# Another written order for the first 48 steps of attention → rational FFN → relu² FFN, with dummy matmuls in front of 16 groups on TensorE

## The chip, the cores and the metric

One core of one Trainium2 chip. Its engines are named as the profile names them: PE (TensorE matmul) with its weight loads PEld, DVE (VectorE), ACT (ScalarE), POOL (GpSimd) and SP (SyncE, which here only issues DMAs). The metric is the device time of one launch in microseconds; lower is better. Before the change it is 1639.45 us, the median of three runs (1637.97 to 1639.97).

## The reference

Three stages, all in float32 accuracy (the FFN weights arrive as float64):

```python
# attention in chunks of 64 tokens; 8 batches x 8 heads, 576 tokens, head dim 64
scores = (q_c @ k_c.T) / sqrt(64);  scores -= max(scores)
attn = exp(scores) / (sum(exp(scores)) + 1e-9);  x = attn @ v_c      # -> 4608 x 512
# FFN 1, rational; w_in 512 x 2048, w_out 2048 x 512
h = x @ w_in
g = (a0 + a1*h + a2*h**2 + a3*h**3) / (1 + |b0|*|h| + |b1|*h**2 + 1e-6)
x = g @ w_out
# FFN 2, relu squared
x = (s * relu(x @ w_in2)**2 + b) @ w_out2
```

## The kernel before, in words

Attention is done in *units* of 128 tokens. A unit n goes through these steps, each one letter of an order list: `P`/`L` load q, k and v; `T` transposes q and k on PE; `q`, `k` copy them out of PSUM on ACT; `S` makes the scores on PE; `sa`, `sb` (row maxima) and `sc`, `sd` (subtract) on DVE; `e` the exponential on ACT; `ma` to `mc` the sum and its reciprocal on DVE; `n` the normalisation, on POOL, or on DVE where it is written `nD`; `A` a transpose on PE and `a` its copy on ACT; `V` the product with v on PE; `v` the high part of the result on ACT (line 416) and `u` the low part on DVE (line 424). From unit 8 on, `X` transposes q and k on DVE (line 327) in place of `T`. Four units make a block of 512 tokens.

A number is kept as a high part and a low part, so a product is three PE passes. The weights of FFN 1 are prepared tile by tile (16 tiles of each matrix): `w` loads a float64 tile, `f` takes its words apart on ACT (lines 445 and 449), `ga` to `gd` join two tiles' bits on DVE (456, 460, 463), `c` adds on POOL (466), `d` makes the high part on ACT, and the low part (477) is made on DVE (`D`) or POOL (`G`).

A *step* i of FFN 1 is one token block with one 128-column tile of the hidden layer: `M` (lines 530 to 532, twelve 128x512 matmuls), then on three engines `B`, `t`, `l`, `E`, `H` (ACT), `ba`, `bb`, `Na`, `Nb`, `Nc` (DVE: 657, 659, 679, 681, 683), the denominator `r` (634 and 637 on POOL; `p` puts its first half on ACT), the low part `y` of the result (697, on POOL, or on DVE as `yD`), and `R` (line 548, twelve matmuls with w_out). Three PSUM banks hold the hidden values, so `M` of step i waits for `Nc` of step i-3. Steps 0 to 7 use token block 0, 8 to 15 block 1, and step 16 is the first of block 2, which needs units 8 to 11.

Nothing schedules at run time: each engine works through its instructions in program order, and that order is written out by hand-made lists. `START` covers steps 0 to 47 and units 0 to 16; after it `LOOP` covers steps 48 to 127, and `TURN` and a planner cover the change to FFN 2. `play(START)` walks the list and calls the function of each letter; each engine's instruction order is the order in which its letters stand. A letter may end in a mark that names an engine or, for PE groups, the PSUM banks.

Of the kernel before, what the change touches and what calls it, by code (L numbers as in the profile page):

```python
# [33 lines left out]
    "w0 w1A f0 P4 w2 f1 P1 g1Pa g1Pb g1Pc c0 d0 T4a L1A T1x q1 k1 g1Pd D0 f2 S1y s1b c1 d1 w3 q4 s1d s1a k4 w4 w5 "  # L34
    "f3 P3 S4b s1c e1 s4b g3Pa g3Pb s4d T3d G1 g3Pc g3Pd m1a c2 m1b m1c P2 f4 c3 n1D f5 w6A d2 g5Pa P5 q3 s4a g5Pb "
    "P0 d3 s4c w7 g5Pc x0 e4 m4a g5Pd A1a k3 T2b c4 c5 a1 V1a S3x q2 s3b k2 d5 s3a d4 G3 s3c S2b s3d e3 w8 v1 D4 "
    "s2b L4 u1 T5d s2a G2 k5 G5 q5 L3A T0x q0 w9 s2c k0 S5a m4b S0x m4c s2d s5a n4 s5b f6 m3a P6 m3b A4d a4 s5c w10 "
    "s0a m3c s0b s5d f7 V4d s0d L0 g7Pa n3 f8 g7Pb g7Pd s0c e2 e5 A3b m5a P7A e0 f9 a3 g7Pc v4 T6b m0a q6 m5b g9Pa "
    "m5c V3c k6 c6 g9Pb n5D m2a w11 g9Pc m0b u4 m0c w12 n0D w13 Q8 c8 A5b S6a s6b L5 L2A c7 L6 T7b w14 d6 a5 w15 "
    "m2b d7 v3 m2c k7 q7 g9Pd s6a c9 s6d s6c e6 D7 m6a A0d u3 a0 d8 w16 Q9 d9 n2 S7b m6b G6 A2a a2 V2a s7a m6c f10 "  # L40
    "v2 u2 V0c v0 L7 G8 f11 u0 M0 w17 f12 g11Pa o8 M1 o9 g11Pb w18 f13 g11Pc G9 g11Pd t0 n6 c11 w19 g13Pa B0 c10 p0 "
    "r0h Q10 A6c d11 M2 s7b w20 b0a g13Pb t1 B1 p1 W0 b0b X8 b1a l0 V5a r1h E0 g13Pc s7c c12 s7d b1b e7 t2 S8b M3 "
    "N0a d10 l1 d12 s8a G11 a6 G12 m7a v5 B2 N0b f14 m7b E1 D10 N0c m7c b2a u5 n7 A7x b2b g13Pd r2 H0 s8b V6a M4 "
    "N1a s8d y0 f15 N1b v6 s8c l2 N1c t3 u6 H1 c13 g15Pa E2 b3a Q11 R0 B3 d13 N2a e8 a7 y1 g15Pb N2b D13 M5 N2c r3 "
    "B4 X9 p4 r4h t4 b3b R1 l3 M6 g15Pc g15Pd c14 H2 l4 y2 E3 f16 b4a N3a f17 b4b E4 N3b V7y c15 B5 p5 r5h m8a d14 "
    "G14 N3c g17Pa H3 t5 d15 B6 l5 y3 v7 R2 N4a N4b m8b t6 N4c g17Pb o10 b5a m8c b5b E5 n8 u7 g17Pd A8c c17 p6 r6h "
    "N5a a8 H4 N5b w21A M7 f18 l6 Q12 B7 f19 d17 S9y o11 D15 N5c g17Pc y4D c16 H5 s9a b6a s9c g19Pa b6b G17 s9b E6 "
    "R3 d16 p7 r7h g19Pb t7 y5D M8 g19Pc R4 t8 N6a b7a N6b s9d B8 X10 G16 l7 b8a N6c f20 f21 r8 o12 R5 g19Pd M9 c19 "
    "e9 b7b H6 E7 b8b g21Pa N7a t9 y6 B9 c18 m9a l8 N7b p9 r9h E8 N7c w22A H7 d19 g21Pb R6 m9b g21Pc M10 b9a d18 "
    "N8a l9 b9b c20 N8b m9c B10 y7D g21Pd E9 t10 N8c p10 N9a R7 M11 b10a c21 j7 i7 H8 N9b B11 b10b S10b N9c V8a n9 "  # L50
    "O7 r10h y8 w23A d21 s10a s10b X11 l10 s10c A9y v8 M12 s10d a9 e10 u8 V9b G18 S11a E10 t11 m10a N10a H9 G19 r11 "
    "w24 m10b v9 w25 w26 m10c B12 N10b n10 N10c s11a o13 l11 s11b s11d s11c Q13 u9 b11a f22 e11 d20 m11a f23 t12 "
    "m11b b11b E11 A10y H10 g23Pa M13 b12a r12 g23Pb m11c a10 t13 N11a N11b B13 R8 y9 l12 R9 N11c g23Pd V10y y10 "
    "n11 R10 g23Pc v10 M14 H11 A11x c23 b12b b13a p13 r13h E12 u10 b13b l13 N12a M15 E13 N12b t14 N12c y11 B14 D20 "
    "R11 H12 c22 d22 N13a a11 N13b N13c y12 V11y R12 b14a d23 t15 b14b w27A r14 H13 b15a l14 B15 D23 E14 N14a G22 "
    "v11 G21 u11 N14b M16 M17 r15 N14c b15b f24 f25 g25Pa l15 g25Pb y13D E15 g25Pd B16 r16 N15a f26 g25Pc R13 t16 "
    "f27 N15b M18 N15c g27Pa B17 H14 y14 b16a b16b H15 p17 r17h l16 t17 b17a E16 b17b N16a N16b l17 y15D c25 c24 "
# [24 lines left out]
)
# [1530 lines left out]
```

## Time and profile before

| | |
|---|---|
| median of 3 runs | 1639.45 us |
| the profiled execution's own time | 1639.77 us |
| its span | 1638.0 us |
| PE busy | 1586.5 us (97%) |
| DVE, ACT, POOL busy | 82%, 69%, 37% of the span |
| step 0 starts on PE | 60.84 us |
| step 48 starts on PE | 353.0 us |

The span is what the hardware profiler saw of one execution, from the first instruction to the last; the time around it (1.8 us) is launch and end. "Busy" is the union of an engine's instructions. Matmuls are pipelined and their ends modelled, so the distance between two starts says more than a duration: in a dense stretch one 128x512 matmul starts 0.227 us after the other, and a step (`M` and `R`) takes 5.44 us of PE. The column PEclk is the clock granted to TensorE as a share of full speed; its two levels are 1.2 and 2.4 GHz.

### The profile page before, as it was taken

The page shows a single profiled execution, that of the slowest core. Times are in us where ns is not written, and L with a number is a line of the kernel's source. Part 1 is how long each engine was busy: PE and PEld are TensorE (multiplying, and loading weights), DVE is VectorE, ACT ScalarE, POOL GpSimd, SP SyncE. Part 2 cuts the span into 40 slices and gives each one's busy share as a digit, 9 for nine tenths or more (in the row PEclk, how much of TensorE's full clock was granted, in tenths as well). Part 3 has the DMA queues.
Part 4 walks back from the last instruction along what each step waited for, and adds up shares of the span by engine and source line. Part 5 has one row for each costly group of instructions (what it writes and reads, how often), then busy time and mean ns, then how long its engine had stood idle before and what let it go on. Part 6 is the DMA issues. An engine that isn't in the chain of part 4 may idle for free.

```text
span 1638.0 us, 26407 instructions
## 1 busy us (share of the span) xinstructions
PE 1586.5 (97%) x9068; PEld 1293.9 (79%) x9068; DVE 1338.1 (82%) x2165; ACT 1128.0 (69%) x1909; POOL 608.8 (37%) x513
## 2 busy tenths in 40 slices
PE   4699999999999999999999999999999999999998
PEld 3577887777878888888888788888888888888886
DVE  6899988899888988888779987668867886788676
ACT  5788766667677686867678776657665756676554
POOL 3677565347577676757557510000000000000000
PEclk9799999999999999999999999999999999999999
DMA  9655302344263553625034587865589649666853
GB/s 232 158 158 147 93 1 65 84 113 134 66 167 87 154 141 83 196 65 133 3 123 135 206 272 238 324 231 174 164 208 303 233 130 297 213 220 161 279 169 86
DMA packets 365526, 263.93 MB, mean 161 GB/s; under 512 B 276816, under 2 KB 315728, under 8 KB 364880
## 3 DMA queue, kind: packets, MB, share of 16 engines
q1 hardware_dynamic: 352720, 255.55, 53.0%
q10 hardware_dynamic: 12672, 6.69, 1.5%
q8 instruction: 72, 1.18, 0.3%
q14 instruction: 62, 0.51, 0.1%
HBM read 201.33 MB, written 60.82 MB: 160 GB/s over the span
## 4 chain that ended last, share of the span: by engine, by line
PE 79%; DVE 6%; DMA 4%; ACT 4%; issue 3%; POOL 2%; SPq 2%; ACTq 0%; DVEq 0%; POOLq 0%
PE acc L548 20%; PE ae L1107 16%; PE hA L1046 11%; PE h L530 7%; PE h L532 6%; PE h L531 6%; PE hE L1046 5%; PE hc L1046 3%; PE hc L1107 3%; DMA wst<-in_moe_w_in_dram 1%; SPq L269 1%; DMA vs<-in_v_dram 1%; PE pat L383 1%; DVE ah L679 1%; PE pat L408 1%
## 5 line engine op out<-in xcount | busy, mean ns | idle before, releaser
L1107 PE MATMUL ae<-gs,wo 128*128 128x512 f32 x1152 | 294.0, 391 | 1.7 <-DVE acc L1126 0.7
L548 PE MATMUL acc<-gh,w 128*128 128x512 f32 x1152 | 288.0, 392 | 0.0
L530 PE MATMUL h<-xh,w 128*128 128x512 f32 x640 | 256.1, 400 | 8.9 <-DVE t L683 8.0
L1107 PEld LDWEIGHTS ae<-gs,wo 128*128 128x128 f32 x1152 | 215.8, 188 | 49.5 <-DVE acc L1126 1.1
L531 PE MATMUL h<-xl,w 128*128 128x512 f32 x640 | 251.0, 392 | 0.0
L532 PE MATMUL h<-xh,w 128*128 128x512 f32 x640 | 251.0, 392 | 0.0
L548 PEld LDWEIGHTS acc<-gh,w 128*128 128x128 f32 x1152 | 214.1, 188 | 44.4 <-ACT gh L691 0.2
L637 POOL TENSOR_TENSOR r<-r,ah 128x512 f32<-128x512 f32 x130 | 174.3, 1341 | 77.6 <-ACT r L632 65.0
L1046 PE MATMUL hA<-xs,wi 128*128 128x512 f32 x768 | 195.6, 390 | 0.7 <-ACT g L1057 0.7
L697 POOL TENSOR_TENSOR gl<-t,gh 128x512 fp32r<-128x512 f32 x111 | 147.7, 1333 | 100.0 <-ACT gh L691 58.4
L1046 PEld LDWEIGHTS hA<-xs,wi 128*128 128x128 f32 x768 | 144.1, 188 | 31.8 <-ACT g L1057 1.1
L1085 DVE TENSOR_TENSOR gs<-g,gs 128x512 fp32r<-128x512 f32 x224 | 146.4, 684 | 15.1 <-ACT gs L1081 14.5
L548 PE MATMUL acc<-gl,w 128*128 128x512 f32 x576 | 154.8, 390 | 2.0 <-POOL gl L697 1.9
L1081 ACT ACTIVATE gs<-g 128x512 fp32r<-128x512 f32 x224 | 132.7, 624 | 28.2 <-DVE g L1077 27.8
L530 PEld LDWEIGHTS h<-xh,w 128*128 128x128 f32 x640 | 121.2, 189 | 39.1 <-DVE t L683 12.4
L532 PEld LDWEIGHTS h<-xh,w 128*128 128x128 f32 x640 | 121.0, 189 | 26.0
L531 PEld LDWEIGHTS h<-xl,w 128*128 128x128 f32 x640 | 121.2, 189 | 24.2 <-DVE xl L424 0.3
L623 ACT ACTIVATE t<-h,a_sb 128x512 f32<-128x512 f32 x144 | 111.1, 773 | 38.1 <-PE h L532 18.1
L548 PEld LDWEIGHTS acc<-gl,w 128*128 128x128 f32 x576 | 107.6, 188 | 26.5 <-POOL gl L697 4.2
L679 DVE SCALAR_TENSOR_TENSOR ah<-r,h 128x512 f32<-128x512 f32 x144 | 98.1, 681 | 37.1 <-ACT h L668 35.7
L1128 DVE TENSOR_TENSOR acc<-ae,acc 128x512 f32<-128x512 f32 x112 | 77.0, 689 | 61.3 <-PE ae L1107 60.3
L663 ACT ACTIVATE ah<-r,lnb 128x512 f32<-128x512 f32 x144 | 103.6, 719 | 32.8 <-POOL r L637 26.5
(143 smaller groups left out, 2964.9 us busy)
## 6 DMA issues: line engine op xcount, KB each, us to landing
wi<-wq SPq DMA_DIRECT2D x112, 512.0 KB, 4.3
wo<-wq SPq DMA_DIRECT2D x112, 512.0 KB, 4.8
wst<-in_moe_w_in_dram SPq DMA_DIRECT2D x28, 512.0 KB, 5.3
wst<-in_moe_w_out_dram SPq DMA_DIRECT2D x27, 512.0 KB, 4.7
wi<-wp SPq DMA_DIRECT2D x16, 512.0 KB, 4.0
wq<-wc SPq DMA_DIRECT2D x32, 256.0 KB, 2.8
w<-wi SPq DMA_DIRECT2D x16, 512.0 KB, 6.6
raw<-x2d SPq DMA_DIRECT2D x16, 512.0 KB, 7.4
```

Source lines behind the costliest of these rows:

```text
L530: T.matmul(h, wh, xh[:, kk], start=kk == 0, stop=False)
L531: T.matmul(h, wh, xl[:, kk], start=False, stop=False)
L532: T.matmul(h, wl, xh[:, kk], start=False, stop=kk == KD - 1)
L548: T.matmul(o, l, r, start=first and n == 0, stop=last and n == 2)
L623: A.activation(t1, h_t[i], AF.Identity, scale=a_sb[:, 3:4], bias=a_sb[:, 2:3])
L637: eng.tensor_tensor(out=r, in0=r, in1=ah, op=ALU.mult)
L679: V.scalar_tensor_tensor(out=t, in0=r, scalar=ONE, in1=y, op0=ALU.add, op1=ALU.mult)
L697: (eng or (G if i < N1 else V)).tensor_tensor(out=gl, in0=tmp.pop(i)["g"], in1=f(g_t[i][0]), op=ALU.subtract)
L1046: T.matmul(ps[b], w[:, l, z * P:(z + 1) * P], x[:, z], start=n == 0 and p in (1, 2, 5), stop=n == 5, skip_group_check=True)
L1081: A.activation(gx[t, s, k][0][:, 0], gt[t, s, c], AF.Copy)
L1085: V.tensor_tensor(out=g[:, 1], in0=gt[t, s, c], in1=f(g[:, 0]), op=ALU.subtract)
L1107: T.matmul(o, w[:, e, l, dp * P:(dp + 1) * P], gx[t, 2 * u + e, k][0][:, g], start=n == 0 and p in (1, 2, 5), stop=n == 5, skip_group_chec ...
```

## The change

The text of `START` is replaced by another order of nearly the same letters. Some letters change their mark, which moves work between engines. Counted over the whole list: `D` (weight low part on DVE) 13 → 6 and `G` (on POOL) 19 → 26; `nD` 6 → 1 and `n` 11 → 16; `yD` 15 → 10 and `y` 32 → 37; `p` (first half of the denominator on ACT) 19 → 13 and `r` on POOL alone 25 → 31; v loads issued from ACT (`LA`) 3 → 0, of 4 DMAs each; the parameters' load `x` moves from the middle of the first loads to the front of SP's queue. The second of the two ACT operations of `f` (line 449) becomes a letter of its own, `h…b`. New is `+`: so many transposes of the identity by itself into a PSUM bank that nothing reads, 172 in 16 groups (26, 31, 1, 17, 6, 6, 6, 10, 9, 6, 3, 9, 8 and 12 ahead of step 0, 20 ahead of step 3 and 2 in front of the first `R`).

```diff
 START = (
-    "w0 w1A f0 P4 w2 f1 P1 g1Pa g1Pb g1Pc c0 d0 T4a L1A T1x q1 k1 g1Pd D0 f2 S1y s1b c1 d1 w3 q4 s1d s1a k4 w4 w5 "
...
+    "w0A w1A x0 f0 h0b f1 P1 g1Pa h1b g1Pb g1Pd +26c T1b w2 f2 g1Pc w3 k1 c0 f3 c1 P2 w4 q1 g3Pa d1 g3Pb h3b d0 "
+    "+31c T2d h2b S1a k2 q2 w5 D0 g3Pd f4 g3Pc f5 h5b P0 G1 h4b P5 +1h S2b s1a +17c T0d s1b s1c s1d q0 g5Pa P4 w6 "
...
+    def heat(n, x):
+        if x in "ab":
+            to = ps_a.tile([P, 2, TB], F32, tag=f"acc{'ab'.index(x)}", name="heat")[:, 0]
+        elif x == "x":
+            to = ps_a.tile([P, TB], F32, tag="att", name="heat")
+        else:
+            to = h_bank("cdh".index(x))
+        for _ in range(n):
+            T.transpose(to[:, 0:P], ident, ident)
...
-            w_ends(st, w)
+            w_abs(st, w)
+            if phase:
+                w_low(st)
...
-        do["h"] = lambda n, _: w_get(n)
+        do["h"] = lambda n, x: w_low(words[n][3]) if x else w_get(n)
```

The lines of the new kernel stand 7 to 11 lower, so line 477 is 484 there, 316 is 327, and so on.

PE, from the program's start, before (line 316 is `T`, 339 is `S`, 383 is `A`; `h` and `pat` are PSUM banks):

```order
L316 MATMUL pat<-ident,qk 128x128 x12
L316 MATMUL h<-ident,qk 128x128 x4
L339 MATMUL pat<-qk,vq 64x64
L339 MATMUL h<-qk,vq 64x64 x2
L339 MATMUL pat<-qk,vq 64x64 x2
```

PE at the same place, now (line 319 is the new dummy transposes, 327 is `T`, 350 is `S`):

```order
L319 MATMUL h<-ident 128x128 x26
L327 MATMUL pat<-ident,qk 128x128 x8
L319 MATMUL h<-ident 128x128 x31
L327 MATMUL h<-ident,qk 128x128 x8
L350 MATMUL pat<-qk,vq 64x64 x16
L319 MATMUL h<-ident 128x128
L350 MATMUL pat<-qk,vq 64x64 x16
L319 MATMUL h<-ident 128x128 x17
```

The dummies need only `ident`, which is made at the start, and stand in front of groups that wait for a load.

DVE, the end of the first attention units, before (368, 371 and 373 are `ma`, `mb`, `mc`, 377 is `nD`):

```order
L463 SCALAR_TENSOR_TENSOR w<-wst,w 128x512 x2
L368 TENSOR_REDUCE sm<-e 128x8
L371 TENSOR_SCALAR sm<-sm 128x8
L373 RECIPROCAL sm<-sm 128x8
L377 TENSOR_TENSOR e<-e,sm 128x512
```

DVE at the end of the first attention units, now (379, 382 and 384 are `ma`, `mb`, `mc`, 360 and 367 are the maxima and subtractions of other units):

```order
L379 TENSOR_REDUCE sm<-e 128x8
L382 TENSOR_SCALAR sm<-sm 128x8
L367 TENSOR_TENSOR e<-pat,mx 128x4x64 x2
L384 RECIPROCAL sm<-sm 128x8
L379 TENSOR_REDUCE sm<-e 128x8
L360 TENSOR_REDUCE mx<-pat 128x4 x2
```

The normalisation no longer follows the reciprocal on DVE; it stands on POOL.

POOL, around the first results of the steps, before (634 and 637 are `r`, 697 is `y`, 466 is `c`, 377 is `n`, 477 is `G`):

```order
L634 TENSOR_SCALAR r<-ah,ab_sb 128x512
L637 TENSOR_TENSOR r<-r,ah 128x512
L697 TENSOR_TENSOR gl<-t_878,gh 128x512
L466 TENSOR_TENSOR w<-w,wst 128x512
L697 TENSOR_TENSOR gl<-t_934,gh 128x512
L634 TENSOR_SCALAR r<-ah,ab_sb 128x512
L637 TENSOR_TENSOR r<-r,ah 128x512 x2
L466 TENSOR_TENSOR w<-w,wst 128x512
L697 TENSOR_TENSOR gl<-t_974,gh 128x512
```

POOL at the first results of the steps, now (641 and 644 are `r`, 704 is `y`, 473 is `c`, 388 is `n`, 484 is `G`):

```order
L641 TENSOR_SCALAR r<-ah,ab_sb 128x512
L644 TENSOR_TENSOR r<-r,ah 128x512
L484 TENSOR_TENSOR w_7_1271<-w,w_7_1271 128x512
L704 TENSOR_TENSOR gl<-t_1084,gh 128x512
L704 TENSOR_TENSOR gl<-t_1130,gh 128x512
L641 TENSOR_SCALAR r<-ah,ab_sb 128x512
L644 TENSOR_TENSOR r<-r,ah 128x512
L473 TENSOR_TENSOR w<-w,wst 128x512 x2
L644 TENSOR_TENSOR r<-r,ah 128x512
L704 TENSOR_TENSOR gl<-t_1167,gh 128x512
L388 TENSOR_TENSOR e<-e,sm 128x512
L704 TENSOR_TENSOR gl<-t_1314,gh 128x512
```

A weight tile's low part (484) now stands on POOL right ahead of the first `y`, and each `y` has more of POOL's work in front of it.

## Rows read from the trace of the kernel before

**Rows 1.** Windows by stage: columns in the header line.
```profile
core 0: us, PE busy (x) PEld busy (x) DVE busy (x) ACT busy (x) POOL busy (x), PEclk, DMA share, GB/s
0.00:60.80 60.80, 31.47 (x504) 24.15 (x504) 42.38 (x87) 37.77 (x73) 27.70 (x27) 0.87 0.87 216
60.80:88.00 27.20, 21.23 (x165) 16.61 (x166) 23.97 (x43) 21.41 (x40) 17.79 (x15) 0.80 0.54 124
88.00:353.00 265.00, 261.76 (x1645) 211.27 (x1644) 233.96 (x386) 195.91 (x330) 162.65 (x131) 1.00 0.35 94
353.00:1638.00 1285.00, 1272.06 (x6757) 1041.89 (x6755) 1037.80 (x1652) 872.86 (x1470) 400.65 (x342) 1.00 0.57 173
```

**Rows 2.** Timeline of PE: start, us, line, names, [idle before <-releaser].
```profile
77.43 0.79 PE L530 MATMUL h<-xh,w 128*128 128x512 f32 x1 [3.41 <-DVE t L683]
...
85.12 0.50 PE L530 MATMUL h<-xh,w 128*128 128x512 f32 x1 [1.53 <-DVE t L683]
```

**Rows 3.** Windows, the stretch from 75 to 150 us.
```profile
75.00:150.00 75.00, 69.15 (x532) 55.69 (x533) 73.40 (x133) 65.38 (x118) 57.91 (x46) 0.95 0.53 132
```

**Rows 4.** Groups by line on DVE, 0 to 353 us: busy us, mean ns | idle before.
```profile
L659 DVE SCALAR_TENSOR_TENSOR t<-t,a_sb,h 128x512 f32<-128x512 f32 x47 | 34.7, 740 | 1.1 <-ACT ah L617 0.7
...
L477 DVE TENSOR_TENSOR w<-w,w 128x512 fp32r<-128x512 f32 x13 | 12.7, 976 | 2.0 <-ACT w L473 2.0
...
L327 DVE STREAM_TRANSPOSE qkT<-qk 128x512 f32<-128x512 f32 x18 | 11.7, 684 | 0.0
...
L697 DVE TENSOR_TENSOR gl<-t,gh 128x512 fp32r<-128x512 f32 x14 | 11.0, 787 | 0.0
...
L377 DVE TENSOR_TENSOR e<-e,sm 128x512 f32<-128x512 f32 x5 | 5.3, 1051 | 0.1
```

**Rows 5.** Timeline of DVE, the last low part of block 2.
```profile
162.40 0.41 DVE L424 TENSOR_TENSOR xl<-pat,xh 128x256 fp32r<-128x256 f32 x1
```

**Rows 6.** Timeline of PE, step 16's first matmul and step 14's `R`.
```profile
163.32 0.39 PE L530 MATMUL h<-xh,w 128*128 128x512 f32 x1
...
174.21 1.98 PE L548 MATMUL acc<-gh,w 128*128 128x512 f32 x8
```

**Rows 7.** Groups by line on POOL, 0 to 353 us.
```profile
L637 POOL TENSOR_TENSOR r<-r,ah 128x512 f32<-128x512 f32 x44 | 59.7, 1356 | 27.3 <-ACT r L632 23.1 <-DVE t L657 2.1
...
L697 POOL TENSOR_TENSOR gl<-t,gh 128x512 fp32r<-128x512 f32 x32 | 43.3, 1354 | 37.7 <-ACT gh L691 18.9 <-PE acc L548 11.7 <-DVE e L356 5.2
L477 POOL TENSOR_TENSOR w<-w,w 128x512 fp32r<-128x512 f32 x19 | 25.7, 1368 | 6.4 <-ACT w L473 5.7 <-POOL w L466 0.7
...
L377 POOL TENSOR_TENSOR e<-e,sm 128x512 f32<-128x512 f32 x11 | 12.0, 1087 | 5.4 <-DVE sm L373 4.7 <-ACT gh L691 0.7
```

**Rows 8.** Windows, from step 0 to step 14's `y`.
```profile
60.80:172.00 111.20, 103.34 (x763) 83.15 (x764) 105.53 (x183) 95.12 (x168) 82.42 (x65) 0.95 0.52 138
```

**Rows 9.** Timeline of POOL, step 14's `y`.
```profile
170.88 1.30 POOL L697 TENSOR_TENSOR gl<-t,gh 128x512 fp32r<-128x512 f32 x1 [1.12 <-ACT gh L691]
```

**Rows 10.** Timeline of ACT and its DMA issues (ACTq), 11 to 15 us.
```profile
11.69 2.97 ACTq L282 DMA_DIRECT2D vq<-in_v_dram  x4
14.70 0.60 ACT L320 ACTIVATE vq<-pat 128x512 f32<-128x512 f32 x1 [2.39 <-PE h L316]
```

**Rows 11.** Timeline of SP, one of the parameters' four loads.
```profile
27.09 0.43 SPq L1432 DMA_DIRECT2D a_sb<-in_moe_a_dram  x1
```

**Rows 12.** Timeline of PE, 128x128 transposes early and later.
```profile
26.01 1.08 PE L383 MATMUL pat<-ident,e 128*128 128x128 f32 x4 [2.46 <-DVE e L377]
...
27.83 1.94 PE L316 MATMUL pat<-ident,qk 128*128 128x128 f32 x8 [0.74 <-PE pat L383]
...
31.71 0.66 PE L316 MATMUL h<-ident,qk 128*128 128x128 f32 x4
...
53.25 1.09 PE L316 MATMUL pat<-ident,qk 128*128 128x128 f32 x8 [1.57 <-ACT eT L393]
```

More of the change, by code (lines that the diff above doesn't have):

```diff
@@ L449, in w_low @@
         A.activation(low, low.bitcast(U32), AF.Copy, scale=2.0 ** -29)
-    def w_ends(st, w):
-        w_abs(st, w)
-        w_low(st)
     def w_clamp(st, w, eng=V):
@@ L1437, in tile_chunk_attention__then__rational_ffn__then__relu2_ffn @@
             "w": lambda n, x: w_stages(n // (2 * MF), 1, A if x else SP), "x": lambda n, x: params(A if x else SP),
-            "T": att_T, "q": lambda n, _: att_T_out(n, 0), "k": lambda n, _: att_T_out(n, 1),
+            "+": heat, "T": att_T, "q": lambda n, _: att_T_out(n, 0), "k": lambda n, _: att_T_out(n, 1),
             "X": lambda n, _: att_turn(n), "S": att_S, "s": att_S_out, "e": lambda n, _: att_exp(n),
```

94 rows, old and new, of the table START are left out of this document.

## The prediction

> **What bounds the kernel now.** I read the windows by stage first, then PE's own waits, then the engines that PE waits for. In the windows [rows 1] the reader is to compare the length of each stretch with PE's busy time. From 353 us on PE is busy for 1272 of 1285 us, and that part of the program is the same text before and after, so it only moves as a whole. From 88 to 353 us PE is busy for 261.8 of 265.0 us. So 3.2 us can be had there. Ahead of that lie the idle times: 60.80 − 31.47 = 29.3 us before step 0 and 27.20 − 21.23 = 6.0 us from step 0 to 88 us, together 35.3 us. What a new order of the first 48 steps can give is in that start, and in keeping it afterwards.
>
> What PE waits for after step 0 is seen in its timeline [rows 2]: step 3 sat idle for 3.41 us and step 4 for 1.53 us, both for a DVE instruction of line 683, the `Nc` of steps 0 and 1, which frees the PSUM bank. DVE itself does not wait then: in the 75 us from 75 to 150 it is busy for 73.40 us, while ACT is busy for 65.38 and POOL for 57.91 us [rows 3]. So between step 0 and about step 16 DVE's order decides: an instruction less ahead of a milestone on DVE brings the milestone forward by about its duration, as long as ACT and POOL follow.
>
> **The change, part by part.**
>
> *Until step 0.* Step 0 needs the low part of the last unit of block 0. That unit is 0 before and 3 now; in both lists the low part's second half is the 86th instruction on DVE. DVE was busy for 42.38 of the 60.80 us up to there [rows 1]. Same count, nearly the same kinds: three normalisations leave, and a pair of DVE transposes and other units' work take their place. I put 0 on this and take step 0 at the same place, before the two corrections that come below (ACT's issues, the dummies).
>
> *From step 0 to step 16.* Step 16 is the first that needs block 2, and the last thing it needs is the low part of unit 11. I counted DVE's instructions up to it in both lists: 253 before, 246 now. Out go three normalisations (units 0, 1, 5), four weight low parts (tiles 10, 15, 20, 23) and three `yD` (steps 4, 5, 7); in come the two transposes of unit 12 and one line 659. By the mean durations [rows 4] this is 3 × 1.05 + 4 × 0.98 + 3 × 0.79 = 9.4 us out and 2 × 0.68 + 0.74 = 2.1 us in: 7.3 us less. The milestones between agree in sign: `Nc` of step 1 is DVE's 121st instruction before and the 115th now, that of step 8 the 195th and the 178th. Before, unit 11's low part starts its last half at 162.40 us [rows 5] and step 16 starts at 163.32 us [rows 6], so step 16 stood right behind it and its time moves with it. If DVE stays as full as it was, step 16 comes 7.3 us earlier.
>
> *What POOL has to take.* All ten of these operations now stand on POOL. Up to `y` of step 14 POOL's list has 93 instructions in place of 85: three normalisations, three low parts and three `y` more, one line 637 fewer; by POOL's means [rows 7] 3 × 1.09 + 3 × 1.37 + 3 × 1.35 − 1.36 = +10.1 us. From step 0 to that `y` POOL was busy for 82.4 of 111.2 us, 28.8 us idle [rows 8]. The new work therefore needs a third of that idle time, and if the stretch also shrinks by 7.3 us only 28.8 − 10.1 − 7.3 = 11.4 us are left of 104: POOL would be 89% busy, in order, with each idle piece a wait for ACT or DVE. I do not believe that all of it can be had. Behind a late POOL instruction stand the weights' `c` and the denominators, for which ACT's `l` and then DVE's `N` wait. Bounds: from 7.3 us gained (POOL keeps up) to a loss of 5 us (the slower rival below). I take 5 of the 7.3 us, near the DVE bound, because DVE is what PE is seen to wait for and POOL had a quarter of the stretch free.
>
> *ACT's issues.* Before, ACT issued twelve v loads. At 11.69 us four of them took 2.97 us, and the copy of a transposed unit behind them began only at 14.70 us, after 2.39 us idle [rows 10]; PE's scores waited for that copy. The profile names PE as the releaser, but the issues end just before the copy starts. The new list issues these loads from SP. In exchange, the parameters' four loads, which SP needed up to 0.43 us each for [rows 11], now stand ahead of the first q load, up to 1.7 us of delay, while the 512 KB weight load that stood ahead of it goes to ACT's queue. Bounds: 0 to 3 us of early idle gone from DVE's 60.80 − 42.38 = 18.4 us. I take 1.5 us.
>
> *The dummies.* A 128x128 transpose costs (1.94 − 1.08)/4 = 0.22 us before 31 us and (1.09 − 0.66)/4 = 0.11 us later [rows 12]: the two levels of the clock, 1.2 and 2.4 GHz, although the column PEclk does not show the lower one there. The 150 ahead of step 0 are 16 us at the upper and 32 us at the lower level, against 29.3 us of idle PE; the 22 others are 2.4 us against 6.0 us. At the upper level they lie in idle time; what they could give back is the groups after them running in half the time, which is no part of the path once DVE is full. I cost them at 0, from a gain of 2 us (DVE waits less for units in the first 60 us) to a loss of 6 us (cold, and in front of groups whose load has landed).
>
> The Trainium skill, "TensorE: Matmul & The Clock Gate", Part 4 on the PE-mode transpose, says that transposes do not count as activity for the clock as matmuls do and do not bring it to full rate. This speaks against the change, whose dummies are transposes. The trace does not settle it: ahead of the first fast transposes at 31.71 us PE ran twelve transposes, but also 64x64 matmuls between them [rows 12]. By that rule the sum would take the lower end of the dummies' range, and the second rival below becomes likely.
>
> *After step 16.* DVE keeps a lead of nine or more instructions, POOL falls further behind its old count (98 before, 110 now, up to `y` of step 18). PE's 3.2 us of waits there may shrink or grow by a part: 0.
>
> *Sum.* 0 − 5 − 1.5 + 0 + 0 = −6.5 us, against the profiled execution's own 1639.8 us (span 1638.0 and 1.8 us around it): 1633.3 us. That execution is within 0.4 us of the median of the runs, so no correction; I say 1633 us.
>
> **Rivals.** *POOL becomes the bound (slower).* The place is `R` of steps 10 to 18. The `y` of step 14 started on POOL at 170.88 us [rows 9] and its `R` on PE at 174.21 us [rows 6], so about 2 us were spare behind its 1.3 us. If POOL's waits stay as long as they were, its 10.1 us come on top, less these 2 us and less the 3 us by which idle pieces close when work is at hand: +5 us, 1645 us. It decides once POOL's idle time in the stretch stays above 28.8 − 10.1 + 2 = 20.7 us. For it: POOL's waits are for ACT, in pieces spread over all steps. Against: 28.8 us is much, and step 14's `R` did not stand right behind its `y`.
>
> *The dummies hold up the start (slower, or no gain).* At the lower level 32 us do not fit into 29.3 us, and the first 57 stand ahead of the second unit's transposes, 12 us of PE. Step 0 is then 3 to 6 us later, DVE's idle time longer by as much, and the 5 us are spent: 1634 + 6 = 1640 us, up to 1645. For it: the rule above. Against: the first 26 (5.7 us) stand where PE has nothing else to do, ahead of the first unit's loads.
>
> *DVE's lead is lost to ACT (same).* ACT was 65.38 of 75 us busy [rows 3], and its own count hardly changes (223 to 220 up to unit 11's high part). If ACT's waits stay, about 2 us remain: 1638 us.
>
> *More than forecast (faster).* POOL keeps up (7.3), and fast PE groups and the free ACT queue take 3 us of early idle time: 1639.8 − 10.3 = 1629.5 us, or down to 1626.
>
> **How the numbers follow.** A difference under 0.2%, 3.3 us, cannot be told from no change by a measurement of this kernel. Forecast (a gain of 3.3 to 8.5 us) 0.42; more than that 0.20; ACT or a half-used lead (within 3.3 us) 0.18; POOL 0.12; dummies or the reordered loads slower than 3.3 us 0.08. So faster 0.62, same 0.18, slower 0.20. The range from 1626 to 1643 us leaves out about 0.07 below and 0.10 above; the likeliest case's own range is 1631 to 1636.5 us.
>
> **What would show it.** Right: step 0 at 57 to 61 us; step 16 at 155 to 159 us; DVE over 93% busy from step 0 to step 16; step 3's and 4's waits together under 4.9 us; POOL's idle time in the stretch under 16 us; line 484 with 6 and line 388 with 1 instruction on DVE up to step 48. The dummies are right if transposes run at 0.11 us before 15 us. Wrong: step 0 after 63 us (the dummies or the loads), PE waiting for line 704 on POOL for more than 3 us in all (POOL), or DVE with over 8 us of idle time between step 0 and 16 with waits for ACT.

## The result and the profile after

The changed kernel takes 1649.98 us (median of 5 runs, 1648.22 to 1651.44) against 1639.82 us of the kernel before, run beside it (5 runs, 1637.97 to 1639.97). The ratio is 1.0061, 95% interval 1.0050 to 1.0073: slower by 10 us, where 6.5 us of gain were forecast. The profiled execution of the changed kernel has 1651.44 us, its span 1649.7 us.

Where the time went is first seen in the windows with the bounds of [rows 1] (us from and to, length, busy time of PE, PEld, DVE, ACT, POOL with instructions, granted clock, DMA share, GB/s):

```profile
0.00:60.80 60.80, 45.26 (x590) 39.81 (x590) 34.08 (x76) 36.88 (x70) 28.58 (x28) 0.86 0.84 199
60.80:88.00 27.20, 19.64 (x207) 15.74 (x211) 20.07 (x39) 16.77 (x33) 15.11 (x12) 0.87 0.50 122
88.00:353.00 265.00, 256.56 (x1577) 206.74 (x1577) 225.98 (x362) 191.75 (x321) 180.30 (x151) 0.99 0.36 92
353.00:1649.70 1296.70, 1283.73 (x6875) 1052.65 (x6873) 1046.73 (x1673) 880.20 (x1482) 405.31 (x347) 1.00 0.58 173
```

The first row already holds most of it: in the first 60.80 us DVE did 34.08 us of work and not 42.38 [rows 1]. PE's 45.26 us there are no gain, they contain the dummies. Cut at step 0 and step 16 instead, the kernel before and then the changed kernel read:

```profile
0.00:60.84 60.84, 31.47 (x505) 24.16 (x505) 42.42 (x87) 37.81 (x73) 27.75 (x27) 0.86 0.87 216
...
60.84:163.32 102.48, 94.66 (x724) 75.96 (x725) 96.99 (x170) 86.55 (x154) 77.32 (x62) 0.95 0.56 149
```
```profile
0.00:69.93 69.93, 48.84 (x686) 42.73 (x687) 40.45 (x89) 39.30 (x74) 32.04 (x31) 0.84 0.81 192
...
69.93:179.85 109.92, 99.48 (x716) 77.81 (x715) 93.26 (x159) 85.25 (x151) 83.27 (x67) 0.96 0.51 131
```

Step 0 starts at 69.93 us (60.84 before), step 16 at 179.85 us (163.32 [rows 6]), step 47 at 356.5 us (343.9), and the span is 11.7 us longer. DVE is idle 29.5 us before step 0 and 16.7 us between step 0 and step 16. Before it was 18.4 and 5.5 us. Between the two steps DVE now waits mainly for ACT, 12.3 us in all (engine, line, releaser: us in all, times, longest; before, the waits for ACT are 2.5 and 1.5 us):

```profile
DVE w L463 <- ACT w L456: 5.1, 1, 5.1
DVE ah L686 <- ACT h L675: 3.1, 4, 2.3
DVE t L664 <- ACT ah L624: 2.3, 1, 2.3
...
DVE xl L435 <- ACT xh L427: 1.8, 1, 1.8
```

The late step 0 is a story of SP's queue. In SP's timeline (start, us, line; L283 loads v, L270 loads q and k of unit 8 in 16 pieces, L447 a weight) the reader is to see four v loads that take 7.54 us to issue, twelve that take 15.72 us, then unit 8, and behind unit 8 the v loads of units 3 and 5:

```profile
25.81 7.54 SPq L283 DMA_DIRECT2D vq<-in_v_dram  x4
33.47 0.53 SPq L447 DMA_DIRECT2D wst<-in_moe_w_in_dram  x1
...
35.69 15.72 SPq L283 DMA_DIRECT2D vq<-in_v_dram  x12
51.45 5.02 SPq L270 DMA_DIRECT2D qk<-in_q_dram  x8
56.52 3.91 SPq L270 DMA_DIRECT2D qk<-in_k_dram  x8
60.47 5.21 SPq L283 DMA_DIRECT2D vq<-in_v_dram  x8
65.79 0.54 SPq L447 DMA_DIRECT2D wst<-in_moe_w_in_dram  x1
```

Before, unit 8 was issued from 55.61 to 65.05 us, when v of all four units of block 0 had been issued by 52.03 us, the last of it by ACT:

```profile
49.34 2.69 ACTq L282 DMA_DIRECT2D vq<-in_v_dram  x3
55.61 5.50 SPq L269 DMA_DIRECT2D qk<-in_q_dram  x8
61.15 3.90 SPq L269 DMA_DIRECT2D qk<-in_k_dram  x8
65.10 5.22 SPq L282 DMA_DIRECT2D vq<-in_v_dram  x8
```

There too v of unit 5 stood behind unit 8, but unit 5's product (`V5`) stood behind step 0 on PE. Now `V5` stands in front of step 0. DVE waits for unit 8's k in front of unit 6's subtractions, which free the bank that unit 7's scores want; PE waits for DVE, then for v of unit 5, and step 0 is right behind (DVE's row, then PE's rows of the same trace):

```profile
62.25 0.71 DVE L338 STREAM_TRANSPOSE qkT<-qk 128x512 f32<-128x512 f32 x1 [2.94 <-DMA qk<-in_k_dram]
```
```profile
64.08 0.69 PE L350 MATMUL pat<-qk,vq 64*64 64x64 f32 x32 [3.73 <-DVE e L367]
...
68.45 1.55 PE L419 MATMUL pat<-eT,vq 64*64 64x64 f32 x30 [2.27 <-DMA vq<-in_v_dram]
69.93 0.79 PE L537 MATMUL h<-xh,w 128*128 128x512 f32 x1
```

ACT stands in one load for 4.63 us: the issue of weight 10 on its own queue. (Weight loads change their queue too: those of weights 0, 10, 11 and 31 went from SP to ACT, those of 6, 21 to 23 and 27 to 30 from ACT to SP.) DVE waits 4.0 us for the exponential behind it, and POOL 6.7 us for the reciprocal that DVE makes of its sums.

```profile
37.56 4.63 ACTq L447 DMA_DIRECT2D wst<-in_moe_w_in_dram  x1
42.24 0.63 ACT L373 ACTIVATE e<-e 128x512 f32<-128x512 f32 x1 [5.13 <-issue]
```

### The profile page after: what moved, and what is told of

Read it like the earlier page. It is cut to its first block, busy times and chain, and to the rows that moved or that the text cites. A ratio compares the mean times of both kernels' runs of the same rounds, so it can differ in the third digit from the quotient of the medians.

```text
span 1649.7 us, 26796 instructions
## 1 busy us (share of the span) xinstructions
PE 1605.2 (97%) x9240; PEld 1314.9 (80%) x9240; DVE 1326.9 (80%) x2148; ACT 1125.6 (68%) x1903; POOL 629.3 (38%) x536
## 4 chain that ended last, share of the span: by engine, by line
PE 81%; DVE 4%; DMA 4%; SPq 3%; POOL 3%; issue 3%; ACT 2%; DVEq 0%; POOLq 0%; ACTq 0%
PE acc L555 21%; PE ae L1114 16%; PE hA L1053 11%; PE h L537 7%; PE h L539 7%; PE h L538 7%; PE hE L1053 5%; PE hc L1053 3%; PE hc L1114 2%; DMA wst<-in_moe_w_in_dram 2%; SPq L270 1%; SPq L283 1%; DMA wst<-in_moe_w_out_dram 1%; POOL r L644 1%; PE pat L419 1%
## 5 line engine op out<-in xcount | busy, mean ns | idle before, releaser
L644 POOL TENSOR_TENSOR r<-r,ah 128x512 f32<-128x512 f32 x130 | 172.0, 1324 | 66.7 <-ACT r L639 55.6
L704 POOL TENSOR_TENSOR gl<-t,gh 128x512 fp32r<-128x512 f32 x116 | 153.2, 1323 | 96.6 <-ACT gh L698 67.2
```

What stands on the lines that cost most here:

```text
L644: eng.tensor_tensor(out=r, in0=r, in1=ah, op=ALU.mult)
L704: (eng or (G if i < N1 else V)).tensor_tensor(out=gl, in0=tmp.pop(i)["g"], in1=f(g_t[i][0]), op=ALU.subtract)
```

## The experiments

All times are medians; a ratio is against the kernel before on the same chip. "Step n" is the start of its first matmul on PE in the profiled execution, in us.

| run | step 0 | step 16 | step 47 | time | ratio, 95% |
|---|---|---|---|---|---|
| before | 60.8 | 163.3 | 343.9 | 1639.8 | |
| changed | 69.9 | 179.9 | 356.5 | 1650.0 | 1.0061 (1.0050 to 1.0073) |
| no_dummies | 66.8 | 176.3 | 353.0 | 1651.1 | 1.0074 (1.0057 to 1.0091) |
| q8_late | 60.0 | 171.5 | 348.2 | 1645.0 | 1.0038 (1.0025 to 1.0051) |
| v_on_act | 69.3 | 177.6 | 354.3 | 1648.6 | 1.0055 (1.0040 to 1.0070) |
| loads_all | 69.9 | 178.4 | 355.1 | 1649.1 | 1.0057 (1.0040 to 1.0073) |
| b_then_a_0 | 69.1 | 183.0 | 359.6 | 1657.5 | 1.0107 (1.0092 to 1.0122) |
| a_then_b_0 | 61.3 | 174.7 | 355.4 | 1648.6 | 1.0056 (1.0041 to 1.0071) |
| b_then_a_16 | 61.3 | 162.8 | 339.9 | 1638.1 | 0.9992 (0.9982 to 1.0001) |
| a_then_b_16 | 62.0 | 171.1 | 354.2 | 1648.9 | 1.0059 (1.0042 to 1.0075) |
| q8_ew | 62.2 | 172.5 | 349.2 | 1642.5 | 1.0013 (1.0004 to 1.0023) |
| q8_ew_s10 | 62.3 | 172.9 | 349.5 | 1643.6 | 1.0026 (1.0014 to 1.0038) |
| q8_no_dummies | 59.9 | 175.2 | 351.8 | 1647.4 | 1.0048 (1.0034 to 1.0063) |
| moves_only | 61.6 | 167.9 | 355.9 | 1652.1 | 1.0075 (1.0058 to 1.0092) |
| q8_moves_back | 61.3 | 175.5 | 360.4 | 1659.3 | 1.0123 (1.0108 to 1.0138) |
| a_then_b_10 | 62.2 | 171.3 | 351.9 | 1645.7 | 1.0041 (1.0026 to 1.0056) |
| b_then_a_28 | 61.6 | 162.6 | 341.5 | 1638.8 | 0.9997 (0.9988 to 1.0007) |
| b_dve_more | 66.7 | 168.5 | 349.3 | 1647.3 | 1.0043 (1.0028 to 1.0058) |
| q8_dve_less | 61.0 | 171.8 | 348.4 | 1643.8 | 1.0027 (1.0018 to 1.0037) |
| act_free | 68.3 | 177.0 | 353.6 | 1649.4 | 1.0059 (1.0042 to 1.0075) |

Each step time is that of one execution. Five runs with q8_late's list up to step 0 (q8_late, a_then_b_16, q8_ew, q8_ew_s10, a_then_b_10) have step 0 between 60.0 and 62.3 us, so 2 us in one column can be chance.

**Dummies or loads.** The first four runs take the dummies out, and move loads in three ways.

> The changed kernel with its 16 groups of dummy matmuls left out, nothing else edited. Theory 'loads' (the new order of the start's loads on SP makes the attention late): the dummies fill TensorE's waits, so step 0 stays at 69 to 72 us and the time at 1649 to 1653 us. Theory 'dummies' (they hold real matmuls up): step 0 comes 6 us or more earlier, at 64 us or before, and the time falls to 1638 to 1644 us.

All `+` letters removed. Step 0 came 3.1 us earlier, half of what "dummies" asked for, and the time did not follow: 1651.1 us, with an interval that lies over that of the changed kernel. Theory "dummies" falls; "loads" has its time right, though not its step 0 at 69 to 72 us.

> The changed kernel with the 16 loads of attention unit 8 (9 us of issues on SP) moved behind the v loads of units 3 and 5 and two weight loads, and unit 8's two transposes on VectorE moved in front of its scores. Theory 'loads': V5 and the conversions of weights 10 to 13 no longer wait, step 0 starts at 63 to 66 us and the time is 1643 to 1647 us. Theories 'dummies' and 'engines' (the moved work of ScalarE, VectorE and GpSimd makes steps 10 to 16 late): step 0 within 2 us of 69.9 us, time within 2 us of 1650 us.

```diff
- ... a1 Q8 T3c ... L3 P7A L5 ... w12 w13 s3d ... g11Pa X8 Q10 ... m6b S8a ...
+ ... a1 T3c ... L3 P7A L5 ... w12 w13 Q8 s3d ... g11Pa Q10 ... m6b X8 S8a ...
```

The 16 loads of one unit and the two transposes that need them, moved together: step 0 at 60.0 us, 9.9 us earlier, step 16 by 8.3 us, the time by 5.0 us. The trace shows weight 12 issued at 55.84 us and unit 8 behind it, and PE in front of step 0 without a wait of note:

```profile
34.55 21.18 SPq L284 DMA_DIRECT2D vq<-in_v_dram  x20
55.84 0.54 SPq L448 DMA_DIRECT2D wst<-in_moe_w_in_dram  x1
56.55 0.37 SPq L453 DMA_DIRECT2D wst<-in_moe_w_out_dram  x1
56.97 5.08 SPq L271 DMA_DIRECT2D qk<-in_q_dram  x8
```
```profile
60.02 0.49 PE L538 MATMUL h<-xh,w 128*128 128x512 f32 x1 [0.32 <-ACT xh L428]
```

So the place of unit 8's loads and transposes, with `V5` in front of step 0, is shown as the cause of the late step 0 (the run does not part the loads from the transposes). But step 16 is still 8.2 us late with step 0 early: there is a second loss. (In this run and some others lines stand one lower than in the changed kernel.)

> The changed kernel with the v loads of units 1, 0 and 3 issued by ScalarE again, unit 1's at about 12 us, the other two behind them. Theory 'loads': unit 0's values are there before 47 us, so the 2.4 us wait for them on TensorE is gone and SP comes 4 to 5 us earlier to unit 8; step 0 at 64 to 67 us, time 1643 to 1647 us. A rival: ScalarE stands in its own issues, 3 to 8 us of them, and nothing is won: step 0 at 68 to 73 us, time 1648 to 1654 us.

> The changed kernel with the start's loads alone put in another order: the four small parameter loads behind weight 7 instead of first, v of unit 1 on ScalarE at about 12 us, v of unit 0 ahead of weight 8, weights 10 and 11 on SP instead of ScalarE, unit 8 behind weight 13. Theory 'loads': step 0 at 59 to 63 us and the time 1636 to 1642 us, level with the kernel before. Theory 'engines': step 0 may come earlier, but steps 10 to 16 lose their 7 us still, and the time is 1644 to 1649 us. Theory 'dummies': step 0 stays at 68 us or later.

```diff
  v_on_act
- ... q1 ... k2 ... e0 ... e4 ... (L1, L0, L3 where the changed list has them)
+ ... L1A k2 ... L0A e0 ... L3A e4 ...
  loads_all
- x0 ... k2 ... w7 ... L1 ... w8 ... L0 ... Q8 ... w10A ... w11A ... w13
+ L1A k2 ... w7 x0 ... L0 w8 ... w10 ... w11 ... w13 Q8   (and X8 in front of S8a)
```

Both missed. In v_on_act the rival holds: ACT stood 5.6, 5.0 and 3.1 us in front of exponentials that follow loads on its own queue. In loads_all unit 8 is late too, and still step 0 is at 69.9 us: v of units 1 and 0 went ahead of weights, ACT waited up to 9.6 us for one, and PE 9.2 and 8.5 us for ACT's copies behind it (the 8.5 us in front of a group of dummies). The start takes no single rule such as "v early"; each load has its place among all.

**The stretch behind step 0.** Lists spliced of both orders were to tell whether the second loss lies in the changed order itself.

> A list spliced of both: the order of the kernel before up to step 0, and from there what is left in the changed order. Theory 'middle' (besides the start, the changed order between step 10 and step 16 costs 8 us by itself): step 0 at 60 to 62 us, step 16 at 169 to 174 us, time 1643 to 1648 us. Theory 'start' (what is late in steps 10 to 16 is only a late effect of the changed start): step 16 within 2 us of the 163.3 us of before, time 1637 to 1641 us.

> The other splice: the changed order up to step 0, with unit 8's loads late as in the run before (step 0 at 60.0 us), and from there what is left in the order of before. Theory 'middle': step 16 at 161 to 164 us and the time 1635 to 1640 us, level with before or below it. Theory 'start': step 16 at 169 to 172 us, time 1643 to 1647 us.

> Before's order up to step 16, the changed order from there. The stretch from step 16 on costs nothing or wins a little in the changed kernel (its lag on before falls from 16.6 us to 12.6 us by step 47): the time is 1635 to 1640 us. If the later steps carried part of the loss, it would be 1641 us or more.

> The changed order up to step 16, with unit 8's loads late, then before's order. Theory 'middle': step 16 at 171 to 172 us as with the whole changed order and the time 1644 to 1649 us: the loss is all there by step 16 and before's later order doesn't give it back.

The splices at step 0 missed their times, one of them usefully. In b_then_a_0 the list is that of before up to step 0, with before's loads and no dummies; only what the changed order puts between, `V5` among it, now stands in front of step 0. PE then waits for v of unit 5, which SP issues at 63.73 us behind unit 8's (54.84 to 63.7 us), and step 0 is at 69.1 us: the same cause again. From step 10 to step 16 it takes 50.5 us though its start is in the order of before, which speaks for "middle".

```profile
66.21 0.45 PE L419 MATMUL pat<-eT,vq 64*64 64x64 f32 x2 [7.78 <-DMA vq<-in_v_dram]
```

a_then_b_0 loses 6.6 us at steps 6 and 7, behind a wait of 4.7 us for DVE, and is 11.4 us late at step 16 though the order there is that of before; a splice can cost as much as the thing it looks for, and this one settles nothing. The two at step 16 agree with each other. With before's order up to step 16 and the changed one from there, step 16 is at 162.8 us and step 47 at 339.9 us, 3.9 us ahead of before; the reverse comes to step 47 6.0 us later than q8_late. So from step 16 to step 47 the changed order is better, by 3.4 us in the trace, and all that is lost is lost before. b_then_a_16 is the fastest version found, 1638.1 us, but its interval still holds 1.

> Before's order up to step 28, the changed order from there. In the run with the switch at step 16 the lag on before falls by 2.5 us between 250 and 300 us of before's time (steps 32 to 40). If that gain belongs to the changed order of these steps alone: lag -2 to -3 us at step 48 here too, time 1635 to 1639 us. If it needs the earlier change: level with before within 1 us at step 48, 1639 to 1641 us.

2.4 us ahead at step 47 and 1.7 us at step 48. The switch costs 1.7 us at step 28 (0.7 us ahead at step 27, 1.0 us behind at step 28), and 3.4 us are won behind it. In b_then_a_16, step 28 is 0.4 us ahead of before and step 47 3.9 us: what the changed order wins, it wins behind step 28. The time, 1638.8 us, is no different from before.

**Which part loses between step 10 and step 16.** These six steps take 39.7 us before and 47 to 52 us in all runs that keep the changed order in them. 2.7 us of this is one `R` more that stands there (half of a step's 5.44 us). In q8_late PE's waits from 108 to 172 us are many and short (engine, line waited at, releaser: us in all, times, longest):

```profile
PE h L538 <- DVE t L691: 2.2, 1, 2.2
PE h L538 <- DVE e L368: 1.3, 1, 1.3
PE h L538 <- DVE xl L436: 0.9, 1, 0.9
PE pat L395 <- ACT o L596: 0.8, 1, 0.8
PE acc L556 <- DVE e L368: 0.7, 1, 0.7
PE h L538 <- ACT w L481: 0.4, 1, 0.4
```

Before has one such wait in the like stretch, 1.4 us for POOL. The first of q8_late's, 2.2 us, stands ahead of step 10 and so outside the six steps; within them PE is idle for 48.97 − 44.77 = 4.2 us, before for 39.72 − 38.32 = 1.4 us. PE is also slower in them. Soon behind the wait of 2.2 us the granted clock falls to 0.50, the level of 1.2 GHz, and a 128x512 matmul then starts 0.43 us after the other and not 0.23 us. Before, it is 1.00 all the way. These are the six steps of q8_late, the 3.40 us in them, and the six steps of before:

```profile
122.56:171.53 48.97, 44.77 (x360) 34.20 (x361) 41.78 (x71) 35.95 (x65) 36.54 (x31) 0.97 0.43 108
123.80:127.20 3.40, 3.40 (x17) 2.24 (x18) 2.62 (x5) 1.80 (x4) 3.32 (x4) 0.50 0.20 31
```
```profile
123.60:163.32 39.72, 38.32 (x349) 31.05 (x348) 37.56 (x68) 33.15 (x61) 31.30 (x27) 1.00 0.53 149
```

Of the 9.2 us that q8_late needs more, 2.7 us are the `R`, 2.8 us more idle time and up to 1.7 us the half clock (half of 3.40 us, an estimate); about 2 us are not accounted for.

> The run with unit 8's loads late, and two single instructions of ScalarE moved: the absolute value of step 8 (B8) in front of VectorE's two passes of steps 7 and 8, and that of step 11 (B11) in front of VectorE's first pass of step 11. In the traces of the changed order ScalarE stands 3.0 and 2.6 us in these two, waiting for VectorE, with GpSimd behind it. Theory 'wrong place' (such instructions in a place from which one engine waits for another in turn make the middle slow): step 10 to step 16 takes 3 to 5 us less than its 48.9 us, time 1640 to 1643 us. Rival 'VectorE is full' (the middle is bound by the sum of VectorE's work and any order of it is late): step 16 within 1 us of 171.5 us, time 1644 to 1647 us.

> As the run before it in this call, and VectorE's two subtractions of unit 10 (which free the PSUM bank that step 11 wants) in front of the copy of the first accumulator instead of behind it and a 1.8 us weight pass. Theory 'wrong place': step 11 starts 2 to 3 us earlier yet, time 1638 to 1642 us. Rival 'VectorE is full': no further change, within 1.5 us.

```diff
- ... d17 b7b b8a B8 l7 ...          - ... b11a V9b N10c b11b y9 s11a w26 B11 ...
+ ... d17 B8 b7b b8a l7 ...          + ... B11 b11a V9b N10c b11b y9 s11a w26 ...
  q8_ew_s10 as well
- ... A9a i7 g21Pa s10c j7 s10d H8 ...
+ ... A9a s10c s10d i7 g21Pa j7 H8 ...
```

Inconclusive. The 2.2 us wait goes, but others come at the next places, and step 16 is no earlier:

```profile
PE pat L395 <- POOL e L389: 2.3, 1, 2.3
PE h L538 <- DVE xl L436: 0.9, 1, 0.9
PE pat L420 <- ACT eT L405: 0.8, 1, 0.8
```

The 2.2 us show between step 6 and step 10 (21.2 us against 23.5 us), ahead of the stretch. Step 0 stands 2.2 us later in this trace with the same list ahead of it, so from step 0 to step 16 it takes 110.3 us against 111.5 us. The time fell from 1645.0 to 1642.5 us, with intervals that just miss each other and on another chip, while the two profiled spans are alike (1642.2 and 1641.9 us). The further move gave nothing.

> The run with unit 8's loads late, without the dummy matmuls. If the dummies do nothing (their 16 groups stand where TensorE waits anyway): time within 1.5 us of the 1645 us with them. If they help by holding the granted clock up in the start: 1646.5 to 1650 us. If they hold real work up: 1640 to 1643.5 us.

1.0048 against 1.0038, with intervals that overlap: by the time the dummies cannot be told from nothing. The traces lean to a help: without them step 16 is 3.7 us later, and between step 0 and step 16 the granted clock is at its lower level for 13.6 us in place of 6.8 us. The 1647.4 us lie where that was to put them.

> The kernel before, its order kept, with the changed kernel's choice of engine for the normalisations, the low halves of the weights and the low halves of g: eight of VectorE's instructions go to GpSimd before step 16, later ones both ways. By the relief of VectorE that the prediction took as 5 us: step 16 at 157 to 161 us, time 1632 to 1637 us. Rival: they come back as waits for GpSimd, step 16 within 1.5 us of 163.3 us or later, time 1638 to 1643 us.

```diff
  before's list, marks only (ahead of step 16; 20 more behind it)
- n1D n5D n0D D10 D15 D20 D23 y4D y5D y7D G22
+ n1  n5  n0  G10 G15 G20 G23 y4  y5  y7  D22
```

(Ten instructions leave DVE ahead of step 16 and one comes, not eight as expected.) The 31 marks together cost 12 us in before's order. The ones that the prediction counted as a relief stand ahead of step 16, and there the kernel is 4.6 us late; 7.4 us more come by step 47, behind the other 20. In the first 62 us PE waits for a normalisation that POOL now does (before, 2.5 us for DVE and 0.5 us for POOL at this place, and step 0 is only 0.8 us later):

```profile
PE pat L394 <- POOL e L388: 4.6, 2, 4.1
```

> The run with unit 8's loads late, and the changed order kept, but the normalisations and the low halves of the weights and of g given back to the engines of the kernel before: before step 16 eight instructions go from GpSimd back to VectorE. Theory 'moves' (the loss of 8 us between step 10 and step 16 is the wait for GpSimd's slower copies of VectorE's work): step 10 to step 16 takes 41 to 45 us instead of 48.9 us, time 1636 to 1641 us. Theory 'order' (the order itself makes the engines wait in turn): step 10 to step 16 stays at 47 to 51 us, time 1643 to 1648 us.

> The changed order up to step 10, with unit 8's loads late (it stands there 1 us ahead of before), then what is left in the order of before. Theory 'order': step 16 within 3 us of the 163.3 us of before, time 1637 to 1642 us. Theory 'debt' (VectorE and ScalarE come to step 10 with less done: 93.2 us of VectorE's work against 101.8 us, and have to make it up behind it in any order): step 16 at 168 to 173 us, time 1643 to 1648 us.

In the changed order the same marks are worth the reverse: given back, steps 10 to 16 take 50.0 us, step 16 is 4.0 us later and the time 14.3 us longer. Theory "moves" falls. (The mark `p` was in no run given back; it changes in five steps ahead of step 16.) In a_then_b_10 step 10 itself comes 5.9 us later than in q8_late: one `R` more stands ahead of it there, and PE waits 3.9 us for `N7c`, which frees its PSUM bank and fell behind the switch. From there before's order takes 42.9 us, 6.1 less than q8_late, of which the `R` is 2.7, and step 16 comes out at the same 171.3 us. By its numbers this is "debt". But of the lag on before at step 16, 8.0 us, 7.5 us stand at step 11, at the seam, so the last three runs test the debt directly.

**Is it DVE's backlog?** At step 0 q8_late has 36.89 us of DVE's work done, before 42.42.

> The kernel before, with the clamps of weight pairs 3, 5, 7 and 9 made three times instead of once (the clamp can be repeated without changing a value): eight more VectorE instructions of 0.61 us, 4.9 us, all before step 0. Theory 'debt' (VectorE's lost time in the start is not caught up by step 16, though TensorE and step 0 need not wait for it): step 0 late by 0 to 3 us, step 16 late by 3 to 5 us, time 1642 to 1645 us. Rival 'slack' (VectorE's 18 us of idle time before step 0 take them up): step 16 late by under 1.5 us, time 1638 to 1641 us.

> The changed order with unit 8's loads late, without the clamps of weight pairs 1 to 13 (part of the computation left out): seven VectorE instructions of 0.61 us, 4.3 us, nearly all before step 0. Theory 'debt': step 16 earlier by 3 to 5 us than 171.5 us, time 1640 to 1643 us. Rival 'order' (step 10 to step 16 is slow whatever VectorE's backlog): step 16 earlier by under 1.5 us, time 1644 to 1647 us.

> The changed order with unit 8's loads late, and the loads of unit 7 and of weights 10 and 11 issued by SP instead of ScalarE (in the changed kernel ScalarE stands 4.6 us in the issue of weight 10, and VectorE waits 2.8 to 4.0 us for its exponentials behind it). Theory 'debt': VectorE comes to step 0 with 3 to 5 us more done than 36.9 us, step 16 at 167 to 170 us, time 1640 to 1644 us. Rival: the loads come later on SP and what VectorE wins is lost to a wait for a weight; step 16 at 170.5 us or later, time 1644 us or more.

```diff
  b_dve_more: before's list          q8_dve_less: q8_late's list
- g3Pa                               - g1Pa g3Pa g5Pa g7Pa g9Pa g11Pa g13Pa
+ g3Pa g3Pa g3Pa   (5, 7, 9 alike)
  act_free: q8_late's list
- P6 ... L0 L2 ... P7A ... w10A ... w11A
+ P6 ... P7 L0 L2 ... w10 ... w11
```

The windows up to step 0 and from step 10 to step 16, of b_dve_more and then of q8_dve_less:

```profile
0.00:66.70 66.70, 33.57 (x504) 26.35 (x504) 47.99 (x95) 37.94 (x73) 28.17 (x27) 0.84 0.82 198
128.70:168.50 39.80, 38.40 (x350) 31.09 (x349) 37.67 (x68) 33.21 (x61) 31.33 (x27) 1.00 0.55 150
```
```profile
0.00:60.98 60.98, 44.63 (x686) 39.57 (x686) 31.96 (x77) 37.90 (x73) 29.11 (x29) 0.89 0.88 213
123.29:171.80 48.51, 44.78 (x361) 34.25 (x361) 41.75 (x71) 36.04 (x65) 36.52 (x31) 0.96 0.43 108
```

In before's order 47.99 − 42.42 = 5.6 us more on DVE made step 0 5.9, step 16 5.1 and the time 7.9 us later: about one for one, "slack" falls. In the changed order 36.89 − 31.96 = 4.9 us less made step 16 no earlier, and PE's waits from 108 to 172 us are those of q8_late to a tenth (2.1, 1.3, 0.8, 0.8, 0.7 us). So "debt" falls: DVE's work ahead of step 0 sets the time of before's order and not that of the changed one. In act_free its rival holds: with these loads on SP, ACT waited 10.8 us for one weight, and step 0 is at 68.3 us.

What stays open: what makes steps 10 to 16 slow. It is not the dummies, the marks of `n`, `D`, `G` and `y`, or DVE's work ahead of step 0. What is left is the order of these steps with its chain of short waits and the clock that falls behind one of them, and no run that mended one place of it made step 16 earlier. The changed order also has more of DVE's work inside the six steps, 41.78 against 37.56 us, and no run took that alone away; in q8_moves_back it is 44.41 us and the six steps are only 1.0 us longer.

## Why the prediction was wrong

**The failed step is "Until step 0 ... I put 0 on this".** It measured +9.1 us. The working counted DVE's instructions and let loads count only by the time of their issue (0.43 us a parameter, 2.97 us for four v loads). It never asked in which order SP's queue now brought what stands in front of step 0 on PE. The order shows it: `V5` ahead of step 0, and unit 8's sixteen loads ahead of v of units 3 and 5 and of weights 12 and 13. DVE's count was the same, as the prediction says, but DVE was idle for 29.5 us on the way and not 18.4 us. q8_late moves unit 8's loads and transposes alone and gets 9.9 us of step 0 and 5.0 us of time back. The prediction named "step 0 after 63 us (the dummies or the loads)" as what would prove it wrong, but gave it 0.08 as a mishap beside the dummies, where it was the main case.

**"ACT's issues", −1.5 us, was not seen, and its sign is not shown.** The change took 2.97 us of issues off ACT's first 15 us, put v on SP, where twelve loads took 15.72 us to issue, and put weights 10 and 11 on ACT, where the first took 4.63 us to issue at a time when the DMA engines were full. But v back on ACT (v_on_act) gave 1.4 us with overlapping intervals, and with the weights and unit 7's loads on SP (act_free) step 0 came 8.3 us later than in q8_late. The trace of before already had a warning: at 2.39 us one weight load held SP for 3.96 us.

**"From step 0 to step 16", −5 us, failed in its condition and measured 109.92 − 102.48 = +7.4 us.** The count was nearly right: up to step 16 DVE's busy time fell from 139.40 to 40.45 + 93.26 = 133.71 us, 5.7 us (7.3 were counted). "If DVE stays as full as it was" did not hold: DVE's idle time grew by 11.1 us ahead of step 0 and 11.2 us behind it. Nor did "as long as ACT and POOL follow": 12.3 of the 16.7 us behind step 0 are waits for ACT, so the sign of the rival "DVE's lead is lost to ACT" (over 8 us of idle time, with waits for ACT) was there; it had been priced at 1638 us. The waits ahead of steps 3 and 4 did shrink, to 1.60 and 0.55 us, as the working asked, and the lead was lost behind them. The premise that DVE decides between step 0 and step 16 was tested in neither order: b_dve_more and q8_dve_less change DVE's work ahead of step 0, where it counts in before's order and not in the changed one. The marks that were counted lose 4.6 us at step 16 in before's order and win 4.0 us there in the changed one: their worth cannot be read from a count in either list.

**"What POOL has to take", +10.1 us, was right in its count and near in size:** up to `y` of step 14 POOL's busy time went from 109.01 to 116.60 us, +7.6 us (up to step 16 from 105.1 to 115.3 us, +10.2). The slower rival's two signs part. POOL's idle time from step 0 to that `y` was 113.29 − 84.56 = 28.7 us, over its 20.7 us; PE's waits for line 704 were 1.2 us in all, under its 3 us. Since giving POOL's work back to DVE made the changed order slower still (q8_moves_back), this rival was not the cause.

**The dummies, 0, were right in the changed kernel** (no_dummies). They do raise the clock: transposes run at 0.11 us before 15 us, as the prediction asked. What this gave back lay in idle time; with the loads in place (q8_no_dummies) they may be worth something, not shown by the time.

**"After step 16", 0, was too low:** the changed order wins about 4 us between steps 16 and 47 (lag 16.5 to 12.7 us), and 3.4 us in b_then_a_16.

The sum then goes, by the traces: 8.3 us at step 16 from unit 8's loads and transposes, 8.2 us from the order up to there, about 4 us given back, which leaves the lag of 12.7 us at step 47. The medians are only 10.2 us apart, of which q8_late gets 5.0 us back: the cause of the first half is shown, that of the second is only narrowed down.

## What to carry to other kernels

Where a change reorders loads, write down for each milestone the loads that it needs and what now stands ahead of them in the same queue; behind a busy queue a load comes when those in front have gone, whatever its own issue takes (here v of unit 5 behind 8.9 us of unit 8's issues). A bound found in one order is a fact of that order and of one stretch of it: test it with a few extra instructions on that engine before a term of a sum is built on it. An order and its choice of engines may only work together, so undo either alone before crediting it.

## What the runs showed of the hardware

Dummy transposes alone brought the clock up. Nothing else ran on PE before 9.50 us in the changed kernel. Four transposes of unit 1 behind the 26 dummies took 0.66 us and the next four 1.12 us, the upper and the lower level as in [rows 12]:

```profile
1.36 5.81 PE L319 MATMUL h<-ident 128*128 128x128 f32 x26 [1.36 <-POOL ident masks.py:199]
9.50 0.66 PE L327 MATMUL pat<-ident,qk 128*128 128x128 f32 x4 [2.34 <-DMA qk<-in_q_dram]
10.62 1.12 PE L327 MATMUL pat<-ident,qk 128*128 128x128 f32 x4 [0.46 <-DMA qk<-in_k_dram]
```

Without the dummies the same group ran at the lower level:

```profile
9.60 2.17 PE L327 MATMUL pat<-ident,qk 128*128 128x128 f32 x8 [9.60 <-DMA qk<-in_q_dram]
```

The rule that the prediction weighed (the Trainium skill, "TensorE: Matmul & The Clock Gate", Part 4) therefore does not hold for these float32 transposes. The profile calls them MATMUL; no row says whether they run in the transpose mode that the page speaks of.

The issue of a DMA can hold its engine for microseconds: one 512 KB load held ACT for 4.63 of the 10.6 us from its issue to its landing (changed kernel), twenty v loads held SP for 21.18 us (q8_late), while the DMA engines were busy (share 1.06 and 0.96 from 40 to 50 us in the two traces). Four v loads took 2.58 us in the kernel before, at 46.89 us. The Trainium skill, "DMA: Bandwidth & Descriptors", "Issuing engines are not separate DMA queues", says that loads issued by any engine run on the same DMA engines, and that issuing from several saves only the issue time, "usually small relative to the DMA itself". ACT's 4.63 us lie inside the 15.72 us in which SP issued twelve v loads, which agrees with the first; that the issue is small does not hold here.
